# Other start addresses for TensorE's operands in the second layer

## The chip, the core and the metric

The kernel runs on one core of a Trainium2 chip. Its time is the device time of one execution in microseconds; three executions gave 1230.68, 1231.10 and 1233.33 us, and their median, 1231.1 us, is the time before. One further execution was profiled: 1234.02 us, of which the trace covers a span of 1232.2 us. All places in the trace below are counted from the start of that span.

## What is computed

An attention with a small state, and behind it two feed-forward layers on 4608 tokens of width 512:

```python
def _moe_ref(x, w1, w2, w3, w_out):          # "first layer", d_ff = 1024
    a = x @ w1
    b = x @ w2
    h = a * b @ w3
    return (h @ w_out).astype(np.float32)

def _moe2_ref(x, w_in, w_out):               # "second layer", d_ff = 2048
    h = x @ w_in
    relu6 = np.clip(h + 3.0, 0.0, 6.0)
    g = h * relu6 / 6.0
    return (g @ w_out).astype(np.float32)
```

## The kernel before

Every large product is made of three matmuls of type F32R: each operand is split into a rounded part (a name that ends in h, or the first half of a pair) and a rest (l), and high times high, high times rest and rest times high are summed in PSUM (`mm3`, `prod`, and the loops in `output`). A matmul has a stationary operand of 128 x 128 (the weights, loaded by a LDWEIGHTS instruction of its own before each matmul) and a moving operand of 128 x 512 (or 128 x 256 for the state rows), read from SBUF.

The second layer begins when the pools of the first are closed. It works on four pairs of token blocks. For each pair `gates` makes the 2x2 block products x @ w_in by seven products instead of eight, in eight rounds n of seven products, each of six matmuls: 336 matmuls of 512 columns. Then `output` makes g @ w_out by seven products of 28 steps v, each of twelve matmuls: 336 again. So the layer has 4 x 336 matmuls in `gates` (line 936) and 4 x 336 in `output` (line 1097). In the last pair the state rows ride along: 8 groups of 24 matmuls of 256 columns in `gates` (tiles xsB and xs, line 936) and 16 groups of 12 in `output` (tile sx, line 1110).

The operands and where they lie:

- **Weights.** `w_load` brings the seven weight tiles of a round from DRAM in two parts, wa (four tiles: A11, S1, S2, S4) and wb (three: S3, A12, A22), each with a high and a low half (wah, wal, wbh, wbl) and two buffers each. They are the first tiles of the pool `pb` on the left side of SBUF. SP's queue issues these loads; a load of unit u + 4 is issued when the last matmul on unit u is done (`w_done`).
- **Moving tiles.** In `gates` they are xc (seven tiles, written by `combos` from the tile r); in `output` they are hl, written from the results g by ACT (line 71) and DVE (line 79) two steps ahead; in the last pair xc's buffers are used in `output` as well (xcj, sx). xc and r are in the pool `xb` on the right side, hl in `pb`.
- **Others in `pb`.** `half` (a constant, of which one column is read), the small tiles m1, m5, u2, c and rl, the staging tile stg, and G, the results of the gates.

Tiles of a pool lie behind one another in the order in which their names first occur. The left side's tiles begin at byte 16512 of a partition, which is 128 modulo 256, and nearly all tile sizes are multiples of 256 bytes; on the right side the tile `pad` of 96 bytes brings the first tile to 128 modulo 256. So before the change every moving tile and every weight tile of both layers' F32R products begins at 128 modulo 256, and the slices that matmuls take of them begin at multiples of 256 bytes from there.

Of the kernel before, what the change touches and what calls it, by code (L numbers as in the profile page):

```python
# [7 lines left out]
F32 = mybir.dt.float32  # L8
# [11 lines left out]
def attn_moe_kernel(tc, xt_d, xn_d, bd_d, wa, wb, wc, wi, wo, out):  # L20
# [32 lines left out]
    def open_pool(key, **kw):  # L53
        es[key] = ExitStack()
        return es[key].enter_context(tc.tile_pool(name=key, **kw))

    def close_pool(key):
        es.pop(key).close()
# [286 lines left out]
    with tc.manual_schedule():  # L345
# [392 lines left out]
        for b in range(B):  # L738
# [7 lines left out]
            if b == B - 1:  # L746
# [7 lines left out]
                xb = open_pool("xb", bufs=1, side=right, reuse_waits="tile")  # L754
# [33 lines left out]
        flush(0)  # L788
        for _ in first:
            pass  # L790
        for key in ("late", "main", "mid", "pers", "bigs"):
            close_pool(key)

# [5 lines left out]
        pb = open_pool("pb", bufs=1, side=left, reuse_waits="tile")  # L799
# [5 lines left out]
        def w_load(u):  # L805

            p, k = divmod(u // 2, 2 * NG)
            ab = u % 2
            if p >= PAIRS:
                return  # L810
            n, o = (3, 4) if ab else (4, 0)
            wu[u] = [pb.tile([128, n, 256], F32R, tag=f"w{'ab'[ab]}{hl}", name=f"w{'ab'[ab]}{hl}", bufs=2) for hl in "hl"]
            for hl, t in enumerate(wu[u]):
                if k < NG:
                    src = swi[k][hl].rearrange("p s k f -> p s (k f)")[:, o:o + n, :]
                else:
                    src = swo[hl].rearrange("p i n e -> p (i n) e")[:, 7 * (k - NG) + o:7 * (k - NG) + o + n, :]
                nc.sync.dma_start(out=t.bitcast(F32), in_=src)

        def w_done(u):  # L820
            wu.pop(u)
            w_load(u + 4)
# [6 lines left out]

        for u in range(4):  # L830
            w_load(u)
        half = pb.tile([128, 64], F32, name="half")[:, :1]
        nc.vector.memset(half, 0.5)

        def add(out_, a, b):
# [18 lines left out]
        def jit_tiles(pool, tag, n, bufs):  # L854
            return [pool.tile([128, 2, 2, 512], F32R, tag=tag, name=tag + "j", bufs=bufs) for _ in range(n)]

        jit_tiles(pb, "hl", 1, 3)


        G = [[pb.tile([128, NG, 512], F32, name=f"g{k}{j}") for j in range(2)] for k in range(2)]  # L860
# [393 lines left out]
```

## Time and profile before

| | |
|---|---|
| median of three executions | 1231.1 us |
| lowest, highest | 1230.68, 1233.33 us |
| the profiled execution | 1234.02 us, span 1232.2 us |
| TensorE busy (matmuls) | 1191.2 us, 97% |
| VectorE, ScalarE busy | 862.7 us (70%), 551.9 us (45%) |
| second layer, first to last matmul | 568.5 to 1225.0 us |

The trace is read in stages, since the first layer (to 568 us) has waits on several engines, and the second has hardly any. A matmul's recorded duration (389 ns for 512 columns) is longer than the distance to the next one, because matmuls are pipelined; what counts for the time is the distance from one start to the next, which is had from the starts in the timeline, or from a long unbroken piece of the chain divided by its number of matmuls.

### The profile page before, as it was taken

Reading aid. Unit: us, or ns where it says so; the run is one execution under the profiler, and the core shown is the slowest. Engines: PE = TensorE matmul, PEld = TensorE weight load, DVE = VectorE, ACT = ScalarE, POOL = GpSimd, SP = SyncE. Lnnn points to the kernel's source line nnn. Section 1 sums busy time; section 2 is a strip of 40 time slices with the busy share of each in tenths; the row PEclk is TensorE's granted clock in tenths of the full one; section 3 lists DMA queues with packets and bytes.
Section 4 is the critical chain, followed back from the end, with each engine's and each line's share of the span. In section 5 each row is a group of like instructions: output and inputs, shape, how many; then the busy total and the mean of one; then the engine's idle time right before and its main releaser. Section 6 shows DMA issues by size and latency. Waiting matters only on the chain.

```text
span 1232.2 us, 17120 instructions
## 1 busy us (share of the span) xinstructions
PE 1191.2 (97%) x6688; PEld 943.4 (77%) x6688; DVE 862.7 (70%) x1220; ACT 551.9 (45%) x809; POOL 44.7 (4%) x59
## 2 busy tenths in 40 slices
PE   5989899999999999999999999999999999999997
PEld 2446676767777777978888888888888888888886
DVE  6976878888888464264767867687666886558483
ACT  3434454655454354244445434454344543334341
POOL 0000000000000000000101001010010100001100
PEclk9989999999999999999999999999999999999999
DMA  9751666485864210134889878998788987445973
GB/s 355 271 203 69 241 222 224 143 313 180 278 199 181 76 50 12 58 111 155 249 258 257 286 230 257 273 253 267 234 266 280 249 263 237 152 148 156 249 226 69
DMA packets 118576, 252.64 MB, mean 205 GB/s; under 512 B 45152, under 2 KB 63072, under 8 KB 111840
## 3 DMA queue, kind: packets, MB, share of 16 engines
q1 hardware_dynamic: 110288, 222.72, 52.6%
q0 software_dynamic: 7632, 27.79, 11.3%
q8 instruction: 52, 0.85, 0.3%
q10 hardware_dynamic: 576, 1.05, 0.2%
q14 instruction: 28, 0.23, 0.1%
HBM read 182.39 MB, written 47.64 MB: 187 GB/s over the span
## 4 chain that ended last, share of the span: by engine, by line
PE 82%; DVE 10%; DMA 4%; ACT 2%; issue 1%; SPq 0%; ACTq 0%; DVEq 0%
PE ps_d L1097 25%; PE ps L936 24%; PE x L88 4%; PE ps_ab L88 4%; PE ps_ab L90 4%; PE x L89 4%; PE x L90 4%; PE ps_ab L89 4%; PE ps_w L419 2%; PE ps_hs L936 2%; PE ps_so L1110 2%; PE ps_p L365 2%; DMA swoh<-sh 1%; DVE sl L79 1%; DMA wal<-swil 1%
## 5 line engine op out<-in xcount | busy, mean ns | idle before, releaser
L936 PE MATMUL ps<-xc,wah 128*128 128x512 f32 x512 | 157.9, 389 | 0.0
L79 DVE TENSOR_TENSOR hlj<-g,hlj 128x1024 fp32r<-128x1024 f32 x84 | 102.4, 1219 | 36.3 <-ACT hlj L71 36.2
L866 ACT ACTIVATE rl<-c,half 128x512 f32<-128x512 f32 x96 | 69.5, 724 | 117.2 <-DVE c L836 67.8
L936 PE MATMUL ps<-xc,wbh 128*128 128x512 f32 x384 | 118.3, 389 | 0.0
L1097 PE MATMUL ps_d<-hlj,wah 128*128 128x512 f32 x384 | 118.2, 389 | 0.0
L88 PE MATMUL ps_ab<-Ah,ph 128*128 128x512 f32 x256 | 105.2, 411 | 10.8 <-DVE pl L79 10.0
L88 PE MATMUL x<-abh,w3ph 128*128 128x512 f32 (+1 forms) x288 | 112.3, 390 | 0.0
L71 ACT ACTIVATE hlj<-g 128x1024 fp32r<-128x1024 f32 x84 | 88.6, 1057 | 52.1 <-PE ps_d L1097 48.2
L936 PEld LDWEIGHTS ps<-xc,wah 128*128 128x128 f32 x512 | 95.7, 188 | 19.5
L89 PE MATMUL x<-abl,w3ph 128*128 128x512 f32 (+1 forms) x288 | 109.0, 378 | 0.0
L90 PE MATMUL x<-abh,w3pl 128*128 128x512 f32 (+1 forms) x288 | 108.9, 378 | 0.0
L90 PE MATMUL ps_ab<-Ah,pl 128*128 128x512 f32 x256 | 102.6, 401 | 1.7 <-DVE pl L79 1.7
L89 PE MATMUL ps_ab<-Al,ph 128*128 128x512 f32 x256 | 102.7, 401 | 0.5 <-DVE Al L79 0.5
L936 PE MATMUL ps<-xc,wal 128*128 128x512 f32 x256 | 99.7, 389 | 0.6 <-DMA wal<-swil 0.6
L1097 PE MATMUL ps_d<-hlj,wbh 128*128 128x512 f32 x288 | 88.7, 389 | 0.0
L529 DVE TENSOR_TENSOR ab<-ps_ab,asb 128x512 f32<-128x512 f32 x64 | 44.0, 688 | 56.7 <-PE ps_ab L90 46.1
L1097 PEld LDWEIGHTS ps_d<-hlj,wah 128*128 128x128 f32 x384 | 72.1, 188 | 14.9
L936 PEld LDWEIGHTS ps<-xc,wbh 128*128 128x128 f32 x384 | 72.0, 188 | 15.0
L71 ACT ACTIVATE abh<-ab 128x512 fp32r<-128x512 f32 (+1 forms) x72 | 43.5, 604 | 77.1 <-DVE ab L529 77.1
L904 POOL DMA_DIRECT2D g<-g x41 | 35.7, 871 | 1102.9 <-DVE c L836 593.9
L936 PE MATMUL ps<-xc,wbl 128*128 128x512 f32 x192 | 74.7, 389 | 0.0
L1097 PE MATMUL ps_d<-hlj,wal 128*128 128x512 f32 x192 | 74.7, 389 | 0.0
(167 smaller groups left out, 2351.5 us busy)
## 6 DMA issues: line engine op xcount, KB each, us to landing
g<-g POOLq DMA_DIRECT2D x41, 512.0 KB, 6.9
wah<-swih SPq DMA_DIRECT2D x32, 512.0 KB, 4.5
wal<-swil SPq DMA_DIRECT2D x32, 512.0 KB, 5.3
wah<-swoh SPq DMA_DIRECT2D x32, 512.0 KB, 4.5
wal<-swol SPq DMA_DIRECT2D x32, 512.0 KB, 5.3
wbh<-swih SPq DMA_DIRECT2D x32, 384.0 KB, 5.1
wbl<-swil SPq DMA_DIRECT2D x32, 384.0 KB, 5.4
wbh<-swoh SPq DMA_DIRECT2D x32, 384.0 KB, 5.3
```

The lines of the kernel that those rows point to most:

```text
L71: nc.scalar.activation(out=out_, in_=in_, func=AF.Copy)
L79: e.tensor_tensor(out=out_, in0=in_, in1=hi.bitcast(F32), op=ALU.subtract)
L88: nc.tensor.matmul(ps, lh, rh, start=first, stop=False)
L89: nc.tensor.matmul(ps, lh, rl, start=False, stop=False)
L90: nc.tensor.matmul(ps, ll, rh, start=False, stop=last)
L365: nc.tensor.matmul(ps[c][32 * q:32 * q + 32, 256 * i:256 * i + 256], st_t[b][r, 2 * c + j, 32 * k:32 * k + 32], w12[mm // 2, 2 * c + j][r, ...
L419: nc.tensor.matmul(w3_ps[m], t[:, o:o + 128], wout[k], start=k == 0, stop=k == M1 - 1)
L529: nc.vector.tensor_tensor(out=ab[:, :n], in0=psb[:, :n], in1=a[:, :n], op=ALU.mult)
L866: nc.scalar.activation(out=rl, in_=c, func=AF.Relu, bias=half, scale=sign / 6.0)
L904: nc.gpsimd.dma_start(out=to, in_=of, accum_op=ALU.add)
L936: nc.tensor.matmul(ps, u[:, k, :], v[:, k, :], start=first and k == 0 and i == 0, stop=k == 1 and i == 2, skip_group_check=True)
L1097: nc.tensor.matmul(d[name][q], a, x[:, k, :], start=i < 3 and n == 0 and z == 0, stop=n == NG - 1 and z == 2, skip_group_check=True)
```

## The change

Four tiles are placed that nothing reads or writes (`shift` in `xb`; `shift3`, `shift1` and `shift2` in `pb`), and `half` is made 64 bytes shorter. No instruction is added or removed, and on no engine does the order change.

```diff
         for _ in first:
             pass
+        xb.tile([128, 32], F32, name="shift")
...
             n, o = (3, 4) if ab else (4, 0)
+            if u == 1:
+                pb.tile([128, 16], F32, name="shift3")
...
-        half = pb.tile([128, 64], F32, name="half")[:, :1]
+        half = pb.tile([128, 48], F32, name="half")[:, :1]
...
+        pb.tile([128, 16], F32, name="shift1")
         jit_tiles(pb, "hl", 1, 3)
+        pb.tile([128, 48], F32, name="shift2")
```

Where tiles begin, modulo 256 bytes, by their sizes in order:

| tiles | before | after |
|---|---|---|
| xc, xcj, sx, r, xs (right side) | 128 | 0 |
| wah, wal | 128 | 128 |
| wbh, wbl | 128 | 192 |
| half | 128 | 192 |
| m1, m5, u2, c, rl, stg | 128 | 128 |
| hl, xsB, gs | 128 | 192 |
| G | 128 | 128 |

The new ends of the tiles reach 64 to 256 bytes further into places that other tiles held before, and with that three instructions' waits differ. Two are DVE's first writes into G, which wait for another set of long landed DMAs. The third is in SP's queue at the start of the second layer: the second buffer of wbl now overlaps by 64 bytes the place of `big7`, a weight tile of the first layer. SP's queue there before (a DMA's row gives its line, the tile it writes and the DRAM tile it reads, its size and what it waits for; DMAHW is a landing of an earlier DMA):

```order
L818 DMA wah<-swih_89 128x1024 [waits DMAHW0_49]
L818 DMA wal<-swil_90 128x1024 [waits DMAHW1_49]
L818 DMA wbh<-swih_89 128x768 [waits DMAHW2_49]
L818 DMA wbl<-swil_90 128x768 [waits DMAHW3_49]
L818 DMA wah<-swih_91 128x1024 [waits DMAHW4_49,PE_49]
```

The same place after:

```order
L821 DMA wah<-swih_89 128x1024 [waits DMAHW0_49]
L821 DMA wal<-swil_90 128x1024 [waits DMAHW1_49]
L821 DMA wbh<-swih_89 128x768 [waits DMAHW2_49]
L821 DMA wbl<-swil_90 128x768 [waits DMAHW3_49,PE_49]
L821 DMA wah<-swih_91 128x1024 [waits DMAHW4_49,PE_49]
```

Nothing moved; the fourth load has a wait on TensorE that it did not have, for the last matmul of the first layer that reads `big7` (line 365).

## Rows read from the trace of the kernel before

**Rows 1.** The page: engines' busy time, and TensorE's clock in 40 slices.
```profile
PE 1191.2 (97%) x6688; PEld 943.4 (77%) x6688; DVE 862.7 (70%) x1220; ACT 551.9 (45%) x809; POOL 44.7 (4%) x59
...
PEclk9989999999999999999999999999999999999999
```

**Rows 2.** The page: the chain that ended last, its shares by engine.
```profile
PE 82%; DVE 10%; DMA 4%; ACT 2%; issue 1%; SPq 0%; ACTq 0%; DVEq 0%
```

**Rows 3.** The same chain in order of time: start, length, what, matmul count.
```profile
85.42 3.43 PE ps_w L419 x8
...
568.63 36.94 PE ps L936 x163
605.56 10.35 DMA wal<-swil
615.96 29.80 PE ps L936 x130
645.76 76.16 PE ps_d L1097 x336
721.92 76.16 PE ps L936 x336
...
1034.72 2.87 PE ps_hs L936 x24
```

**Rows 4.** TensorE's waits: who for whom, total us, times, longest.
```profile
PE ps_ab L88 <- DVE pl L79: 10.0, 6, 3.9
...
PE ps L936 <- DMA wal<-swil: 0.6, 1, 0.6
```

**Rows 5.** Engines' busy time in `output` and `gates` of one pair; clock, DMA share.
```profile
core 0: us, PE busy (x) PEld busy (x) DVE busy (x) ACT busy (x) POOL busy (x), PEclk, DMA share, GB/s
...
645.80:721.90 76.10, 76.10 (x337) 63.03 (x336) 61.52 (x71) 37.40 (x45) 5.77 (x7) 1.00 0.90 266
721.90:798.00 76.10, 76.10 (x338) 63.02 (x337) 48.92 (x74) 32.61 (x49) 6.49 (x8) 1.00 0.82 253
```

**Rows 6.** TensorE's timeline, 256 columns, then 512: start, length, what, count.
```profile
1036.71 0.40 PE L936 MATMUL ps_hs<-xs,wbh 128*128 128x256 f32 x2
...
1037.43 0.63 PE L936 MATMUL ps<-xc,wah 128*128 128x512 f32 x2
1037.90 0.39 PE L936 MATMUL ps<-xc,wal 128*128 128x512 f32 x1
1038.13 0.63 PE L936 MATMUL ps<-xc,wah 128*128 128x512 f32 x2
1038.59 0.39 PE L936 MATMUL ps<-xc,wal 128*128 128x512 f32 x1
1038.82 0.62 PE L936 MATMUL ps<-xc,wbh 128*128 128x512 f32 x2
...
1040.18 0.39 PE L936 MATMUL ps<-xc,wah 128*128 128x512 f32 x1
```

**Rows 7.** TensorE's timeline after its one wait in the second layer.
```profile
615.96 0.50 PE L936 MATMUL ps<-xc,wal 128*128 128x512 f32 x1 [0.64 <-DMA wal<-swil]
616.30 0.64 PE L936 MATMUL ps<-xc,wah 128*128 128x512 f32 x2
616.77 0.40 PE L936 MATMUL ps<-xc,wal 128*128 128x512 f32 x1
```

**Rows 8.** TensorE's timeline in the first layer at the lower clock.
```profile
153.41 0.63 PE L88 MATMUL ps_ab<-Ah,ph 128*128 128x512 f32 x1
...
155.54 0.63 PE L90 MATMUL ps_ab<-Ah,pl 128*128 128x512 f32 x1
```

**Rows 9.** Windows as in rows 5: the stretch of rows 8, with its clock.
```profile
153.41:155.54 2.13, 2.13 (x6) 1.65 (x5) 2.06 (x6) 0.78 (x2) 0.00 (x0) 0.50 1.05 373
```

**Rows 10.** Timelines: TensorE's last matmuls on `big`, then SP's load of wbl.
```profile
544.19 1.09 PE L365 MATMUL ps_p<-big,br 64*32 64x256 f32 x32
...
576.43 0.32 SPq L818 DMA_DIRECT2D wbl<-swil x1
```

## Prediction

> **What bounds the kernel now.** I began with the page's engine line: TensorE's matmuls are busy for 97% of the span, and its clock is granted in full from the middle of the run to its end [rows 1]. The chain that ended last lies on TensorE for 82% [rows 2]. Followed in order of time, its second half is nothing but matmuls: from 645.76 us on, stretches of 336 matmuls in 76.16 us follow each other, the same in `output` and in `gates`, and the one step that is not TensorE's in the second layer is a weight load near 606 us [rows 3]. The list of TensorE's waits says the same: its long waits belong to the first layer (10.0 us on DVE at line 88), and the second has one of 0.6 us, for that load [rows 4]. Beside it DVE is busy for 49 to 62 us of each 76 us and ACT for 33 to 37 us [rows 5]. So from 568.5 to 1225.0 us the time is the number of matmuls times the distance between their starts, and only that distance can be changed by where the operands lie.
>
> **The distance, taken apart.** 76.16 us / 336 = 226.7 ns for 512 columns [rows 3]. Of the state rows, six matmuls of 256 columns stand between 1036.71 and 1037.43 us, 120 ns each [rows 6]. The difference, 106.7 ns, is 256 columns; so 512 columns are 213.3 ns, one column per cycle at 2.4 GHz, and each matmul has 13.3 ns on top, whatever its length. At the lower clock, 1.2 GHz, that part is gone: five starts lie 2.13 us apart, 426 ns each, which is 512 columns at 1.2 GHz and nothing else [rows 8, 9]. So the 13.3 ns is something on the reading side that shows only when the columns are taken at full speed, and each of the 2688 + 384 = 3072 matmuls of the second layer pays it: 3072 x 13.3 ns = 41 us in all.
>
> There is a second thing in the rows. Just after the 256-column matmuls the first six of 512 columns (1037.43 to 1038.82) take 1.39 us, 231.7 ns each, and then the next six (to 1040.18) take 1.36 us, 226.7 again [rows 6]. After the one wait it is the same: the pair from 616.30 to 616.77 us takes 235 ns each [rows 7]. So the 13.3 ns is not simply a constant: moving operand and next weights are read at the same time, their relative timing matters, and after a disturbance the stream needs some six matmuls, 0.03 us in all, to fall back into the pattern of 226.7 ns.
>
> **The change part by part.**
>
> *Instructions.* None is added or moved: 0 us.
>
> *The wait that SP gets.* The fourth load of the second weight set now waits for the last matmul on `big7`. Those matmuls begin at 544.19 us and last 1.09 us; the load is issued at 576.43 us [rows 10]. The wait is over 31 us before, so neither this load nor those queued behind it on SP start later: 0 us. Without that cover the price would be TensorE's wait for weights, as the 0.6 us of [rows 4]. DVE's two first writes into G wait for landings of stores of the first layer, some 10 us old by then: 0 us.
>
> *Other users of the moved tiles.* ACT and DVE write xc and hl at other starts and DMAs write wb and r. Both engines have slack in every stretch, at least 14 us of 76 [rows 5], so even some per cent more in these writes would be covered; the DMAs' share is 0.82 to 0.90 and bytes and descriptors stay the same. 0 us.
>
> *The starts themselves.* Before, the moving tile and the weights of every matmul begin at the same place modulo 256. After it, by the table of the change: xc with wa differ by 128, xc with wb and hl with wa by 64, hl with wb by 0. The tiles of this layer that lie at other multiples of 256 all show 226.7 ns, in `gates` and in `output` [rows 3], but no row has an F32R matmul that begins at another residue. The price has to be bounded.
>
> Bound below: the smallest part on top of the columns that a full-clock row shows. Line 419's matmuls are plain F32 and are recorded as two passes each; eight take 3.43 us, 429 ns each [rows 3], 2 ns above two cycles per column (426.7). There the next weights have twice the time. If all of the second layer came to that, it would gain 3072 x (13.3 - 2) ns = 34.7 us. Bound above: the streams never fall into the pattern, 231.7 ns [rows 6] for 2688 matmuls, 2688 x 5.0 ns = 13.4 us more; with the worst pair, 235 ns [rows 7], 22.3 us more. I take 0, the row nearest to the changed matmuls: the pattern is what the stream settles into by itself, from either side and from starts at every multiple of 256, and what upsets it in the rows is timing, not place. A shift by whole multiples of 64 bytes leaves every small unit of reading (16, 32 or 64 bytes) where it was. That argument fails if reading has a unit of 128 or 256 bytes.
>
> A page of the Trainium skill speaks on this part: "TensorE: Matmul & The Clock Gate", section "Step-by-step: what each phase is for", says that the weights come through a read port of their own and take nothing from the running matmul, and its section "Back-to-back issue gap" gives N / 2.4 + 2.5 ns, an estimate of 215.8 ns here. The rows do not agree: 226.7 ns, and dependent on what came before [rows 3, 6]. By that page the second layer would stand at some 30 us less already, so its sentence on ports can't be used to call the change neutral.
>
> **Sum.** 0 on every part: the profiled execution stays at 1234.0 us, and since it lies 2.9 us above the median of the runs shown, the median stays at 1231.
>
> **The rivals.**
>
> *Faster: the same place is what costs.* If reading goes by units of 64 bytes or more in turn, two streams that begin at the same place of 256 hinder each other, and apart they don't. For: the 13.3 ns is exactly 32 columns of 4 bytes, 128 bytes, a size of that kind, and it is paid with all starts equal. Against: tiles have different starts in time, and in the disturbed rows, where the timing differs, it gets worse and not better. Price: all but the 480 matmuls of hl or xsB with wb change, 2592 x 11.3 ns = 29.3 us, which gives 1202; if only the 1068 that differ by 128 gain, 12.1 us, 1219.
>
> *Slower: the pattern is lost at each change of relation.* The place is TensorE's order of weights: it goes from wa to wb and back within each round (A11 | A22 | S2, S1 | A12, S3 | S4) and similarly in `output`, and since only wb has moved against wa, the difference between moving and weight start changes 298 times in the layer. Before, it never changed. If each change upsets the timing as the 256-column groups do, it costs 0.03 us [rows 6] each: 298 x 0.03 = 8.9 us, 1240; if the stream does not settle at all between two changes, most of them 3 to 12 matmuls apart, 13.4 to 22.3 us, 1244 to 1253. It decides as soon as the settled timing depends on the relation of the starts. For: the settling after each disturbance is in the rows. Against: those disturbances are changes of timing, not of place.
>
> **How the numbers follow.** About 0.2% (2.5 us) is what a measurement of this kernel can tell from no change. No change: 0.42, own range 1228.6 to 1233.6. Faster: 0.26, spread from 1202 to 1228. Slower: 0.32, spread from 1234 to 1253. The likeliest is no change, so 1231. For a range with 8 in 10, I leave out the lower third of the faster case (0.10, below 1212) and the upper third of the slower one (0.10, above 1246): 1212 to 1246.
>
> **What will show it.** The stretches of 336 matmuls: 76.16 us each if I am right; near 73 us for those of xc if the same place is what costs; 77 us and more, with distances that begin to vary after each change between wa and wb, if the pattern is lost. Where xc, hl, wa and wb meet, the four kinds of pairs can be told apart in one trace. The stretches of 24 matmuls of 256 columns show whether the constant (13.3 ns) or the column rate moved. I'd be wrong in the sum if TensorE's waits in the second layer rose above the 0.6 us of now, which would be an effect of the loads and not of the starts.

## The result, and the profile after

The changed kernel takes 1239.57 us in the median, 8.0 us more than before in the same comparison; the ratio is 1.0064 with a 95% interval of 1.0043 to 1.0085. So it is slower, inside the stated range, where no change was forecast.

The profiled execution after spans 1240.0 us, before 1232.2 us. The chain in order of time (start, length, what, number of matmuls) answers to [rows 3]:

```profile
569.05 47.63 PE ps L941 x206
616.68 30.29 PE ps L941 x130
646.98 76.62 PE ps_d L1102 x336
723.59 77.75 PE ps L941 x336
801.35 76.60 PE ps_d L1102 x336
...
1040.64 2.83 PE ps_hs L941 x24
1043.46 9.73 PE ps L941 x42
```

Every long stretch became longer, and each kind by its own amount: `gates` from 76.16 to 77.75 us, `output` from 76.16 to 76.60. The stretches of 256 columns became shorter, 2.83 for 2.87 us. The windows of the same two stretches (length, then busy time and instructions of each engine, clock, DMA share, GB/s) answer to [rows 5]:

```profile
646.98:723.59 76.61, 76.61 (x337) 63.08 (x337) 61.53 (x71) 37.48 (x45) 5.76 (x7) 1.00 0.89 266
723.59:801.34 77.75, 77.75 (x338) 63.08 (x337) 49.62 (x75) 32.62 (x49) 6.49 (x8) 1.00 0.80 245
```

TensorE is busy without a break in both, at the full clock; DVE and ACT have the busy times they had, to within 0.7 us. Nothing waits. The time is in the distances between matmul starts. TensorE's timeline in `output` (start, length, what, count) shows it, where the weights go from wb to wa:

```profile
656.65 0.39 PE L1102 MATMUL ps_d<-hlj,wbh 128*128 128x512 f32 x1
656.88 0.39 PE L1102 MATMUL ps_d<-hlj,wbl 128*128 128x512 f32 x1
657.10 0.62 PE L1102 MATMUL ps_d<-hlj,wah 128*128 128x512 f32 x2
657.57 0.39 PE L1102 MATMUL ps_d<-hlj,wal 128*128 128x512 f32 x1
657.79 0.62 PE L1102 MATMUL ps_d<-hlj,wah 128*128 128x512 f32 x2
658.25 0.39 PE L1102 MATMUL ps_d<-hlj,wal 128*128 128x512 f32 x1
658.48 0.62 PE L1102 MATMUL ps_d<-hlj,wah 128*128 128x512 f32 x2
658.94 0.39 PE L1102 MATMUL ps_d<-hlj,wal 128*128 128x512 f32 x1
659.16 0.62 PE L1102 MATMUL ps_d<-hlj,wah 128*128 128x512 f32 x2
```

From 657.10 to 659.16 us nine matmuls on wa take 2.06 us, 228.9 ns each, three by three in 0.69 us, with no sign of settling to 226.7. Sorted by the kind of pair over `gates` and the first three `output` (the means of all distances between starts where this and the next matmul use the same kind of weights), the changed kernel has:

| moving start, weight start | difference mod 256 | matmuls | mean distance |
|---|---|---|---|
| hl 192, wb 192 | 0 | 384 | 226.8 ns |
| hl 192, wa 128 | 64 | 528 | 229.2 ns |
| xc 0, wb 192 | 64 | 512 | 229.1 ns |
| xc 0, wa 128 | 128 | 703 | 232.7 ns |

In the last line two distances at 616 us are left out, 399 and 335 ns, at the place of the wait of [rows 4]; with them the mean is 233.1 ns, the figure that the expectations below use.

Two pairs with the same difference and different starts have the same distance. That suggested the theory that the runs were made to test: **relation** — what counts is the difference between the starts of the moving operand and of the weights. Against it stood the prediction's own rival (each **change of relation**, at a switch between wa and wb, upsets the timing) and a third theory, **residue** (a moving tile or weights at 0 or 192 are slow or fast by themselves). Residue is already in trouble with the first line: hl and wb, both at 192, have 226.8 ns.

### The profile page after: what moved, and what is told of

It reads as the page before. It is cut to its first block, busy times and chain, and to the rows that moved or that the text cites. A ratio compares the mean times of both kernels' runs of the same rounds, so it can differ in the third digit from the quotient of the medians.

```text
span 1240.0 us, 17119 instructions
## 1 busy us (share of the span) xinstructions
PE 1199.6 (97%) x6688; PEld 942.7 (76%) x6688; DVE 864.4 (70%) x1220; ACT 551.9 (45%) x809; POOL 44.7 (4%) x59
## 4 chain that ended last, share of the span: by engine, by line
PE 83%; DVE 10%; DMA 3%; ACT 2%; issue 1%; SPq 0%; ACTq 0%; DVEq 0%
PE ps L941 25%; PE ps_d L1102 25%; PE ps_ab L88 4%; PE x L88 4%; PE ps_ab L90 4%; PE ps_ab L89 4%; PE x L89 3%; PE x L90 3%; PE ps_w L419 2%; PE ps_so L1115 2%; PE ps_hs L941 2%; PE ps_p L365 2%; DMA swih<-sh 1%; DVE ab L529 1%; PE ps_r L230 1%
## 5 line engine op out<-in xcount | busy, mean ns | idle before, releaser
L941 PE MATMUL ps<-xc,wah 128*128 128x512 f32 x512 | 160.7, 395 | 0.0
```

Source lines behind the costliest of these rows:

```text
L941: nc.tensor.matmul(ps, u[:, k, :], v[:, k, :], start=first and k == 0 and i == 0, stop=k == 1 and i == 2, skip_group_check=True)
```

## The experiments

All differ from the kernel before in start addresses of the second layer alone, in the same way as the change, and stretches in `gates` and `output` are compared with 76.16 us [rows 3]. The lines shown are of the chain in order of time, with its columns as above.

**The change without its step in the weights.** Within `gates` and within `output` every matmul now has the same relation.

```diff
+        xb.tile([128, 32], F32, name="shift")
...
+        pb.tile([128, 16], F32, name="shift1")
         jit_tiles(pb, "hl", 1, 3)
+        pb.tile([128, 48], F32, name="shift2")
```

> The change without shift3: all weights begin at 128 again, xc at 0 and hl at 192. Theory 'relation' (what counts is the difference between the starts of the moving operand and of the weights, modulo 256; from the changed kernel's trace 226.7 ns at 0, 229.1 at 64, 233.1 at 128): a stretch of 336 in gates goes to 78.3 us, one in output to 77.0 us, the whole to about 1244 us, slower than the change itself. Rival 'change of relation' (the rival of the prediction: each switch between wa and wb upsets the timing): within a stretch the relation never changes now, so 76.2 us per stretch and about 1231.5 us.

1241.11 us, ratio 1.0079 (1.0063 to 1.0096).

```profile
644.35 76.92 PE ps_d L1099 x336
721.26 78.08 PE ps L938 x336
```

The rival "change of relation" falls as the source of the loss: nothing changes within a stretch, and the stretches are long all the same. `output` at difference 64 has 76.92 / 336 = 228.9 ns, `gates` at 128 has 78.08 / 336 = 232.4 ns, near the 229.2 and 232.7 of the change. The median is 3 us under what relation gave; the stretches, 0.1 to 0.2 us shorter than expected, make some 1.2 us of that, and the rest is not placed.

**Everything at 0.** Weights and moving tiles all begin at 0; the tile `shift0` lies ahead of the weights.

```diff
+        xb.tile([128, 32], F32, name="shift")
...
+        pb.tile([128, 32], F32, name="shift0")
...
-        half = pb.tile([128, 64], F32, name="half")[:, :1]
+        half = pb.tile([128, 32], F32, name="half")[:, :1]
...
+        pb.tile([128, 32], F32, name="shift1")
         jit_tiles(pb, "hl", 1, 3)
+        pb.tile([128, 32], F32, name="shift2")
```

> All weights and all moving tiles of the second layer begin at 0 modulo 256. 'Relation': difference 0 as before, 226.7 ns, 76.2 us per stretch, 1231.5 us. Rival 'residue' (a moving tile at 0 is slow by itself, or needs weights at 192): above 1235 us, since all 2688 long matmuls now have a start that was slow with both kinds of weights in the changed kernel.

1230.95 us, ratio 0.9993 (0.9982 to 1.0004).

```profile
642.95 76.16 PE ps_d L1100 x336
719.11 76.16 PE ps L939 x336
```

The stretches are the same as before to a hundredth of a microsecond. So a start at 0 costs nothing by itself, and 128 was nothing special: with 0 here and with 192 in the pair of hl and wb above, "residue" falls.

**Weights at 192, moving tiles at 128.** Again `shift0` lies ahead of the weights.

```diff
+        pb.tile([128, 16], F32, name="shift0")
...
-        half = pb.tile([128, 64], F32, name="half")[:, :1]
+        half = pb.tile([128, 48], F32, name="half")[:, :1]
```

> Moving tiles stay at 128, all weights begin at 192: difference 192, that is 64 the other way round. 'Relation', if only the distance counts: 229.1 ns as at 64, 77.0 us per stretch, about 1237.5 us; if the direction counts, another value between 224 and 235 ns, the same in gates and output. 'Residue' (weights at 192 are the better ones, by 2.4 to 4 ns in the changed kernel): below 226.7 ns, about 1222 to 1225 us. 'Change of relation': 1231.5 us.

1247.78 us, ratio 1.0137 (1.0122 to 1.0153).

```profile
647.09 78.40 PE ps_d L1098 x336
725.49 78.40 PE ps L937 x336
```

Both stages have the same distance, 78.40 / 336 = 233.3 ns, as one difference for all demands; it is not the 229.1 of 64. So the direction counts: 64 one way costs 2.4 ns, 64 the other way 6.7 ns. This is twice the loss of the change, from a shift of 64 bytes on one of the two operands.

**Four differences in one trace.** wa at 128, wb at 64, xc at 160, hl at 32, with tiles of the same kind.

> wa at 128, wb at 64, xc at 160, hl at 32: the differences are 32 (xc with wa), 96 (xc with wb), 160 (hl with wa) and 224 (hl with wb), read apart in one trace. 'Relation' in units of 64 bytes: 32 and 224 near 226.7 to 229, 96 and 160 near 229 to 233 ns. 'Residue' or a unit smaller than 64: starts at 32 modulo 64 are slower than all of the changed kernel's, above 233 ns.

1248.50 us, one execution.

```profile
645.92 78.41 PE ps_d L1101 x336
724.33 78.31 PE ps L940 x336
```

Sorted by pairs: 233.5 ns at 32, 233.1 at 96, 233.8 at 160, 233.0 at 224. All four are at the slow end, and 32 and 224, the ones nearest to 0, are no better. The expectation of a unit of 64 bytes was wrong. By itself this run would also fit starts at 32 modulo 64 that are slow alone; the next run has hl at 160 as well, and there its distance goes with the weights, 228.5 ns with wa and 233.4 with wb.

**Sixteen bytes, and four.** wa begins a few bytes into larger tiles; wb and xc stay at 128, hl lies at 160. The run with four bytes has `d = 1`.

```diff
-            wu[u] = [pb.tile([128, n, 256], F32R, ...) for hl in "hl"]
+            e = 0 if ab else 64
+            d = 0 if ab else 4
+            wu[u] = [pb.tile([128, 256 * n + e], F32R, ...)[:, d:d + 256 * n]
+                     .rearrange("p (n f) -> p n f", n=n) for hl in "hl"]
...
+        pb.tile([128, 8], F32, name="shift1")
         jit_tiles(pb, "hl", 1, 3)
+        pb.tile([128, 56], F32, name="shift2")
```

> Looks for the unit, and for a difference that is better than 0. wa begins at 144 (16 bytes into tiles that are 256 bytes larger), wb and xc at 128, hl at 160: differences 240 (xc with wa, 16 the other way), 0 (xc with wb), 16 (hl with wa), 32 (hl with wb). 'Relation in units of 64 or 32 bytes': 240 and 16 read like 0, 226.7 ns. 'Relation down to 16 bytes': 240 and 16 near 233 ns, as 32 and 224 already were (233.8 and 233.0 ns), and only xc with wb stays at 226.7 ns. A difference below 226.7 ns would point to a version that beats both kernels.

1234.67 us, one execution.

```profile
641.78 77.49 PE ps_d L1101 x336
719.26 76.30 PE ps L940 x336
```

> As the run with 16 bytes, but wa begins 4 bytes later, at 132: differences 252 (xc with wa, one column), 0 (xc with wb), 28 (hl with wa), 32 (hl with wb). If the unit is 16 bytes or more, but starts inside a unit are allowed to drift: 252 within 1 ns of 226.7 ns. If every start must be equal to the byte, or a start off the unit costs one more access: above 229 ns.

1244.30 us, one execution.

```profile
645.88 77.87 PE ps_d L1101 x336
723.76 77.67 PE ps L940 x336
```

Sixteen bytes off (xc with wa, `gates`) is nearly free: 76.30 us, 227.1 ns over the stretch. Four bytes off is not: 77.67 us, 231.2 ns. By pairs: 227.5 ns at 240, 228.5 at 16, 233.4 at 32; with four bytes 232.4 at 252, 230.8 at 28, 233.0 at 32. So "relation" holds down to single columns and is not a matter of distance: one column off costs more than four. Neither expectation for the unit was right as a whole. No difference came out below 226.7 ns over a stretch, so none of these points to a version that beats the kernel before.

The pairs at difference 0 are not at 226.7 ns in these two runs: xc with wb has 227.2 ns with sixteen bytes and 229.7 with four. TensorE's timeline in `gates` of the run with four bytes shows why, on twelve matmuls on wb between two groups on wa:

```profile
737.50 0.63 PE L940 MATMUL ps<-xc,wbh 128*128 128x512 f32 x2
737.96 0.39 PE L940 MATMUL ps<-xc,wbl 128*128 128x512 f32 x1
738.19 0.63 PE L940 MATMUL ps<-xc,wbh 128*128 128x512 f32 x2
738.65 0.39 PE L940 MATMUL ps<-xc,wbl 128*128 128x512 f32 x1
738.88 0.62 PE L940 MATMUL ps<-xc,wbh 128*128 128x512 f32 x2
739.33 0.39 PE L940 MATMUL ps<-xc,wbl 128*128 128x512 f32 x1
739.56 0.62 PE L940 MATMUL ps<-xc,wbh 128*128 128x512 f32 x2
740.01 0.40 PE L940 MATMUL ps<-xc,wbl 128*128 128x512 f32 x1
740.25 0.62 PE L940 MATMUL ps<-xc,wah 128*128 128x512 f32 x2
```

Over the 32 such groups in that trace, the first six distances after the switch have a mean of 230.8 ns, the next five 226.8, and the last, before wa, 235 in every case. So here the stream needs some six matmuls to settle after a switch, and the means by pairs contain these.

**One part of the change alone: xc.**

```diff
+        xb.tile([128, 32], F32, name="shift")
```

> One part of the change alone: only the tiles of the right side move (xc, xcj, sx to 0); weights and hl stay at 128. 'Relation': 128 in gates, 0 in output until the last pair: 78.1 us per stretch in gates and 76.2 in output; 1344 + 336 matmuls by 5.8 to 6.4 ns, 9.7 to 10.8 us more, less 0.4 us of the 256-column ones: 1240.5 to 1242.5 us, more than the whole change costs, since wb at 192 brings xc's difference with wb from 128 to 64.

1243.05 us, ratio 1.0085 (1.0062 to 1.0108).

```profile
647.49 76.21 PE ps_d L1098 x336
723.70 78.39 PE ps L937 x336
```

The loss is where the difference is: `gates` at 128 has 233.3 ns, `output` at 0 keeps 76.2 us. The median lies 0.6 us above the expected 1240.5 to 1242.5, with 78.39 us in `gates` for the expected 78.1. And a part costs more than the whole, as expected: in the change, wb at 192 brings xc's difference with wb from 128 down to 64. The ratios of the two overlap in their intervals; it is the second layer in the traces that shows it, 665.9 us from first to last start here and 663.8 in the run that follows.

**The change again,** beside the last three on the same chip.

> The change itself, beside the others on the same chip: 1238 to 1241 us, 77.75 us per stretch in gates and 76.6 in output.

1239.27 us, ratio 1.0061 (1.0039 to 1.0083), with 77.75 us in `gates` and 76.60 in `output`: the stretches of the first profile again.

## Why the prediction was wrong

*What bounds the kernel* was right: after the change the second layer is still one unbroken run of matmuls, and its 7.4 us more between first and last start, of 7.8 us in the span, are distances between starts. By stretches against [rows 3]: 0.8 us in the first pair's `gates` (which lost the wait of [rows 4] and so less), 1.6 us in the second and third each, some 1.4 us in the fourth, 0.4 to 0.5 us in each of three `output` stretches, about 1.2 us in the last `output`, less some 0.5 us in the 256-column ones.

*Instructions, SP's wait, other engines* at 0 were right. SP's queue shows the load that got the wait, at the place where [rows 10] had it at 576.43:

```profile
574.01 0.32 SPq L821 DMA_DIRECT2D wbh<-swih  x1
576.90 0.32 SPq L821 DMA_DIRECT2D wbl<-swil  x1
577.32 0.38 SPq L821 DMA_DIRECT2D wah<-swih  x1
```

It is issued 0.47 us later, in a trace whose second layer begins 0.4 us later, and no wait of TensorE on a weight load is left in the list; at the place of the old one, a single distance of 399 ns remains.

*The starts themselves* is the step that failed: "I take 0". Measured are 2.4 ns more per matmul at difference 64 and 6.0 at 128 (229.1 and 232.7 for 226.7), and with them 7.4 us for the layer. Both reasons for the 0 fell. The first, that the stream settles into 226.7 ns from starts at every multiple of 256, was read from rows that all had difference 0 modulo 256; they could not speak for any other, and I let them. The second, that a shift by multiples of 64 leaves small units of reading where they were, named its own condition for failing (a unit of 128 or 256), but the runs show something else: even 4 bytes matter, and 16 hardly do. The bounds were of use: the upper one by the pair of [rows 7], 235 ns, contains the mean of every kind of pair (226.7 to 233.8), while the milder upper end, 231.7 ns from [rows 6], is exceeded by most.

*The faster rival* (equal starts hinder each other) is refuted for the long matmuls: difference 0 is the best of all that were tried, not the worst. Only the matmuls of 256 columns gain, 2.83 for 2.87 us in 24, or 1.7 ns each. So the reading in the prediction that each matmul pays the same 13.3 ns whatever its length holds at difference 0 alone: at the changed starts the short ones pay less and the long ones more.

*The slower rival* gave 1240 and the median is 1239.57, but that is a coincidence of sums. Its mechanism, a loss at each of 298 switches, is refuted as the source of the loss by the run in which no switch changes the relation and whose stretches are longer still, 78.08 and 76.92 us for 77.75 and 76.60. What it had right is the condition under which it put itself: that the settled timing depends on the relation of the starts. Switches can cost something too, as the timeline of the run with four bytes shows; but in the change, hl with wb has 226.8 ns although every group of them follows a switch. What it had wrong is that the stream settles back to 226.7 ns whatever the starts; at most differences other than 0 it stays slower for as long as the difference lasts. That 1239.57 lies in the stated range is therefore owed to the width of the bounds and not to either rival's mechanism.

The Trainium skill's sentence in "TensorE: Matmul & The Clock Gate" ("Step-by-step: what each phase is for"), that the weight load takes nothing from the running matmul, was set aside in the prediction as not borne out. The runs speak further against it: with clock, columns and instructions the same, moving the weights by 64 bytes made the whole layer slower, 233.3 for 226.7 ns. The formula that the prediction took from the section "Back-to-back issue gap" of that page of the Trainium skill is given there for a single matmul and not for a stream with a weight load before each one, so its 215.8 ns was no figure for this layer.

**What stays open** is why. Shown is that the distance depends on the two starts together, that equal starts are the best of those tried, and that the dependence is fine. Whether it is the weights in use that matter, or those being loaded for the *next* matmul, was not tried by itself, and the switches don't settle it. In the run with four bytes the last of twelve matmuls on wb (xc and the weights in use at 128, the next at 132) takes 235 ns after five of 226.8, which speaks for the next weights; the switch the other way has 225.2 ns over 63 cases, less than the mean of any kind of pair. In `output` of the change the distances at the switches are 226 ns from difference 0 to 64 and 227 ns from 64 to 0, where the next weights alone would give 229 and 227, and the weights in use alone 227 and 229. How the two reads meet in SBUF no trace shows.

## What to carry to other kernels

When TensorE streams F32R matmuls of 512 columns with a new weight load for each, let the moving tiles and the weights begin at the same place modulo 256 bytes; here that was worth up to 1.4% of the whole run, and small tiles ahead of others can break it unseen. To check it, divide an unbroken stretch of the chain by its matmuls and compare stretches that differ in their tiles only. And rows in which a quantity never varies don't show that it is without effect: such a part of a sum gets the whole width of its bounds, and its middle, rather than 0.

## What the runs showed that I had not expected

- Mean distances per 512-column matmul at the full clock, by difference of the starts, without waits: 226.7 ns at 0 where all pairs are at 0; 227.5 at 240 and 228.5 at 16; 228.9 to 229.2 at 64; 230.8 at 28; 232.4 at 252; 232.5 to 233.7 at 128; 233.0 to 233.8 at 32, 96, 160, 192 and 224.
- It is not symmetric (64: 229, 192: 233), and 4 bytes (232.4 at 252) are worse than 16 (227.5 at 240).
- A mean need not be a steady distance: in `gates` with xc alone moved (difference 128), distances of 237.5 and 229.1 ns take turns from 650 us on.
- With 256 columns it goes the other way: 24 of them take 2.87 us at difference 0 and 2.83 us in the change and with weights at 192.
